# FFN gate/up stage: the second row half follows the first by seven matmuls instead of nine

## The chip, the cores and the metric

The kernel runs on one core of one Trainium2 chip. Times are device microseconds (us) of that core. A "before" and an "after" are compared only within the same rounds on the same chip, since the kernel before reads 508.7 us in one set of rounds and 509.1 us in two others.

## The reference, cut to what matters

```python
h  = x + irfft2(rfft2(layernorm(x)) * (w_r + 1j * w_i))          # opening stage, about 80 us
h2 = h + (gelu(layernorm(h) @ w_gate) * (layernorm(h) @ w_up)) @ w_down   # FFN, the rest
# x: 2048 x 576, w_gate and w_up: 576 x 4608, w_down: 4608 x 576, bf16
```

## The kernel before

The change touches only the gate/up stage of the FFN. Rows of x are taken in four blocks of 512 (`tb`), the 4608 features in 36 blocks of 128 (`f`), so there are 144 FFN blocks `m`. The contraction over 576 is cut into pieces of 64 rows. Nine pieces (5 of gate, 4 of up) run on array rows 0-63, the first half; the other nine (4 of gate, 5 of up) run on rows 64-127, the second half. Both halves of a block add into the same two PSUM banks, one for gate, one for up.

`gu(n)` emits first-half matmul `j` of block `n` and second-half matmul `j` of block `n-1` in turn: the second half runs nine matmuls behind the first. I call one such pair a step, and the nine the distance.

```python
ASEQ = [(0, i) for i in range(4)] + [(0, 8)] + [(1, 4 + i) for i in range(4)]  # (bank, weight tile), first half
BSEQ = [(0, i) for i in range(4)] + [(1, 4 + i) for i in range(4)] + [(1, 8)]  # second half
half_done = {}

def gu(n):
    for j in range(9):
        for half, m in ((0, n), (1, n - 1)):
            if not 0 <= m < 144:
                continue
            tb, f = m // 36, m % 36
            o, wt = (ASEQ, BSEQ)[half][j]
            # ... kt, HT
            h0 = 64 * half
            b = 2 * (m % 3) + o                     # six banks: three blocks are in flight
            # the second half enters a bank only after the first half's last matmul there
            aft = [half_done[m, o]] if half and (j == 0 or j == 4) else []
            op = P.op(PE, ... t.matmul(bank(b), WGU[h0:h0 + 64, wt, ...], HT[h0:h0 + 64, kt, :], ...), w=[("PS", b)], after=aft)
            if half == 0:
                half_done[m, o] = op
    m = n - 1
    if m < 0:
        st_N(NT - 1)          # last four matmuls of the opening stage; they need ScalarE's copy GS
        # ...
        return
    # ScalarE: GL = gelu(gate bank);  VectorE: AT[f] = GL * up bank

gu(0)
for tb in range(4):
    for f in range(36):
        gu(36 * tb + f + 1)
        # ... layer norm of the next 512 rows in between
    for p in range(4):
        down(tb, p)           # AT @ w_down, 72 matmuls over the full array
```

`gu(0)` has no second half, so its nine first-half matmuls run alone; nine second-half ones run alone at the end. The `after` of a second-half matmul is a wait of TensorE on itself ("self-wait"): two per block, 288 in all. It sits on the weight load that precedes the matmul.

## Time and profile before

| | before |
|---|---|
| median of 3 runs, us | 508.82 (508.56 to 509.06) |
| span of the profiled run, us | 506.9 |
| TensorE busy | 98% |
| gate/up matmuls in the chain that ended last | 56% |
| down projection in it | 28% |

The first line of the profile page, and its engine table: busy us, share of the span, instructions (PE is TensorE, PEld its weight loads). Below, the head of the chain of work that ended last, by line.

```profile
span 506.9 us, 9999 instructions
## 1 busy us (share of the span) xinstructions
PE 496.6 (98%) x4331; PEld 290.1 (57%) x4331; DVE 182.4 (36%) x376; ACT 157.6 (31%) x296; POOL 46.1 (9%) x61
...
PE PS L740 56%; PE PS L761 28%; PE PS L634 2%; PE PS L649 2%; DMA XO<-in_A_x_dram 1%; PE PS L541 1%; PE PS L579 1%; DVE T_80 L563 1%; ACT U L476 1%; DVE CUS L547 1%; PE PS L558 1%; DVE CUS L548 1%; DVE T_81 L564 1%; DVE U L474 1%; ACT JNK L411 0%
```

The same chain in order of time, its end: start, duration, what ran. L740 is gate/up, L761 down.

```profile
78.62 0.75 PE PS L634 x6
79.87 2.04 PE PS L740 x9
81.91 0.60 PE PS L649 x4
82.51 70.04 PE PS L740 x648
152.55 35.39 PE PS L761 x288
...
398.78 70.04 PE PS L740 x639
468.82 35.40 PE PS L761 x288
```

From 79.87 us to the last matmul the chain is TensorE alone. The `x9` piece is the nine lone matmuls: 2.04 us for half the work of nine steps. Each later stretch holds 648 matmuls, 324 pairs, in 70.04 us, or 216 ns a pair (the last one is 315 pairs and the nine lone second-half matmuls). A lone matmul takes the same 216 ns, so a lone matmul wastes half of its step.

The waits of the weight loads between 79 and 480 us: waiter, released by, us in total, times, longest.

```profile
PEld PS L761 <- issue: 1.7, 4, 0.4
PEld PS L740 <- issue: 1.2, 5, 0.2
PEld PS L649 <- issue: 0.4, 1, 0.4
PEld PS L740 <- ACT GL L752: 0.2, 1, 0.2
```

One weight load waited 0.2 us for ScalarE. No matmul was late for it.

### The profile page before, as it was taken

To read this page: it belongs to the slowest core of one execution; us is meant where nothing else is said; L and a number is where in the kernel's file an instruction comes from. 1 tells how busy PE (TensorE), PEld (TensorE's weight loads), DVE (VectorE), ACT (ScalarE), POOL (GpSimd) and SP (SyncE) were. 2 spreads that over 40 slices of the span, in tenths; PEclk is the share of its full clock that TensorE was granted. 3 is DMA by queue.
4 is the path that set the end of the run, shared out by engine and by line. 5 is a ranking of instruction groups with operands and counts; after the bars stand their busy time and mean duration, and the time that the engine had idled before them with its cause. 6 is when DMAs were issued, how large, how long until landed. Compare 5 with 4: busy or idle time off the path is not lost.

```text
span 506.9 us, 9999 instructions
## 1 busy us (share of the span) xinstructions
PE 496.6 (98%) x4331; PEld 290.1 (57%) x4331; DVE 182.4 (36%) x376; ACT 157.6 (31%) x296; POOL 46.1 (9%) x61
## 2 busy tenths in 40 slices
PE   6899999999999999999999999999999999999997
PEld 2578675444447774444467744444577644444776
DVE  4899673335331114443311134433211233333111
ACT  5788776663230002333310023232200132323000
POOL 3278860000000000000000000000000000000000
PEclk9899999999999999999999999999999999999999
DMA  8679798001100000100000001100000000000000
GB/s 298 151 231 321 246 334 297 1 1 23 25 9 14 17 19 14 23 19 1 1 7 17 19 12 23 25 5 1 1 19 17 13 1 1 1 1 1 13 18 19
DMA packets 25660, 28.64 MB, mean 57 GB/s; under 512 B 11408, under 2 KB 19600, under 8 KB 25488
## 3 DMA queue, kind: packets, MB, share of 16 engines
q1 hardware_dynamic: 23040, 17.39, 11.9%
q0 software_dynamic: 2576, 10.62, 6.3%
q8 instruction: 34, 0.56, 0.5%
q14 instruction: 10, 0.08, 0.1%
HBM read 23.66 MB, written 2.36 MB: 51 GB/s over the span
## 4 chain that ended last, share of the span: by engine, by line
PE 90%; DVE 4%; ACT 2%; DMA 1%; issue 1%; POOL 0%; SPq 0%; DVEq 0%; POOLq 0%
PE PS L740 56%; PE PS L761 28%; PE PS L634 2%; PE PS L649 2%; DMA XO<-in_A_x_dram 1%; PE PS L541 1%; PE PS L579 1%; DVE T_80 L563 1%; ACT U L476 1%; DVE CUS L547 1%; PE PS L558 1%; DVE CUS L548 1%; DVE T_81 L564 1%; DVE U L474 1%; ACT JNK L411 0%
## 5 line engine op out<-in xcount | busy, mean ns | idle before, releaser
L752 ACT ACTIVATE GL<-PS 128x512 bf16<-128x512 f32 x144 | 85.9, 597 | 289.9 <-PE PS L740 289.9
L753 DVE TENSOR_TENSOR AT<-GL,PS 128x512 bf16<-128x512 bf16 x144 | 98.8, 687 | 174.3 <-PE PS L740 172.6
L740 PE MATMUL PS<-HT_69,WGU 64*128 64x512 bf16 x1296 | 144.4, 376 | 0.0
L740 PE MATMUL PS<-HT_84,WGU 64*128 64x512 bf16 x1296 | 144.4, 376 | 0.0
L761 PE MATMUL PS<-WD,AT 128*128 128x288 bf16 x1152 | 141.8, 286 | 0.0
L761 PEld LDWEIGHTS PS<-WD,AT 128*128 128x128 bf16 x1152 | 112.4, 98 | 29.9 <-issue 1.7
L740 PEld LDWEIGHTS PS<-HT_84,WGU 64*128 64x128 bf16 x1296 | 64.5, 94 | 77.9 <-issue 0.5
L740 PEld LDWEIGHTS PS<-HT_69,WGU 64*128 64x128 bf16 x1296 | 64.5, 94 | 76.8 <-issue 0.7
L764 DVE TENSOR_TENSOR OS<-PS,XO 128x288 bf16<-128x288 f32 x32 | 14.6, 457 | 126.0 <-PE PS L761 126.0
L652 DVE SCALAR_TENSOR_TENSOR XO<-PS,XO 128x576 bf16<-128x576 f32 x16 | 12.1, 756 | 11.3 <-PE PS L649 11.3
L541 PE MATMUL PS<-FT,U 128*128 128x290 bf16 x96 | 14.4, 287 | 0.4 <-DVE U L474 0.4
L634 PE MATMUL PS<-DT,V 128*128 128x289 bf16 x96 | 14.5, 287 | 0.2 <-DVE V L587 0.2
L579 PE MATMUL PS<-VT,ZS 128*128 128x256 bf16 x96 | 12.9, 272 | 0.4 <-POOL ZS L568 0.2
L585 ACT ACTIVATE V<-PS 128x768 bf16<-128x768 f32 x15 | 12.0, 810 | 1.1 <-PE PS L579 0.7
L558 PE MATMUL PS<-CUS,BT 128*128 128x289 bf16 (+2 forms) x96 | 10.7, 247 | 1.4 <-DVE CUS L548 1.0
L564 DVE TENSOR_TENSOR T_81<-YS,WS 128x580 bf16<-128x580 bf16 x16 | 11.9, 746 | 0.0
L636 ACT ACTIVATE GS<-PS 128x578 bf16<-128x578 f32 x16 | 10.3, 652 | 5.0 <-PE PS L634 4.9
L561 ACT ACTIVATE YS<-PS 128x578 bf16<-128x578 f32 x16 | 10.5, 654 | 4.5 <-PE PS L558 2.8
L568 POOL TENSOR_TENSOR ZS<-T_81 128x290 bf16<-128x290 bf16 x13 | 11.6, 894 | 1.9
L452 PE MATMUL PS<-ZD 128*128 128x512 bf16 x30 | 10.4, 501 | 1.3 <-POOL ZD L369 1.3
L418 DVE BATCH_NORM_STATS2 ST_53<-XO 128x6 f32<-128x288 bf16 x24 | 9.4, 442 | 4.4 <-DMA XO<-in_A_x_dram 4.4
L541 PEld LDWEIGHTS PS<-FT,U 128*128 128x128 bf16 x96 | 9.2, 98 | 2.9 <-issue 0.8
(61 smaller groups left out, 189.8 us busy)
## 6 DMA issues: line engine op xcount, KB each, us to landing
WD<-in_B_w_down_dram POOLq DMA_DIRECT2D x9, 576.0 KB, 19.7
WGU<-in_B_w_up_dram SPq DMA_DIRECT2D x4, 1152.0 KB, 12.5
WGU<-in_B_w_gate_dram POOLq DMA_DIRECT2D x4, 1152.0 KB, 10.1
out_dram<-OS SPq DMA_DIRECT2D x32, 72.0 KB, 1.6
XO<-in_A_x_dram SPq DMA_DIRECT2D x3, 576.0 KB, 7.7
IT<-c_itab SPq DMA_DIRECT2D x1, 1024.0 KB, 6.7
HT_84<-HN SPq DMA_TRANSPOSE x40, 2.4
XO<-in_A_x_dram SPq DMA_DIRECT2D x2, 288.0 KB, 3.1
```

The costliest lines, as they stand in the source:

```text
L541: P.op(PE, lambda t, b=b, o=o, dt=dt, us=us, g=g: t.matmul(bank(b, 0, 128, 0, 2 * HK), U[:, us, g, :, :], FT[:, o, dt, :], start=(dt == 0) ...
L558: P.op(PE, lambda t, b=b, tb=tb, pl=pl, q0=q0, q1=q1, m=m, sl=sl, sp_=sp_: t.matmul(bank(b, 0, 128, q0, q1), BT[:, sp_, tb, :], CUS[:, sl, ...
L564: P.op(DVE, lambda v, g=g, sl=sl: v.tensor_tensor(T2[:, sl, :, :], YS[:, sl, :, :], WS[:, g, 1::-1, :], op=ALU.mult), r=[("Y", sl)] + wk, ...
L579: P.op(PE, lambda t, b=b, o=o, c=c, zp=zp, sl=sl, sp_=sp_: t.matmul(bank(b, 0, 128, o, o + 256), ZS[:, sl, zp, 128 * c:128 * c + 128], VT[ ...
L585: P.op(ACT, lambda a, g=g, src=src: a.activation(V[:, :, :, g, :], src, ACTF.Copy), r=rk, w=[("V", g, 0)])
L634: P.op(PE, lambda t, b=b, h=h, i=i, kt=kt, c=c: t.matmul(bank(b, 0, 128, 0, K2), V[:, kt, c, :, :], DT[:, 3 * h + i, 0:K2], start=(i == 0) ...
L652: P.op(DVE, lambda v, x2=x2, c=c, sl=sl: v.scalar_tensor_tensor(x2, banks(4 + 2 * sl, 2, 288), 1.0, x2, op0=ALU.mult, op1=ALU.add, accum_o ...
L740: op = P.op(PE, lambda t, h0=h0, kt=kt, wt=wt, f=f, b=b, HT=HT, s=(half == 0 and j in (0, 5)), e=(half == 1 and j in (3, 8)): t.matmul(ban ...
L752: P.op(ACT, lambda a, s2=s2, b0=b0: a.activation(GL[:, s2, :], bank(b0), ACTF.Gelu_apprx_tanh), r=[("PS", b0)], w=[("GL", s2)])
L753: P.op(DVE, lambda v, s2=s2, b0=b0, f=f: v.tensor_tensor(AT[:, f, :], GL[:, s2, :], bank(b0 + 1), op=ALU.mult), r=[("GL", s2), ("PS", b0 + ...
L761: P.op(PE, lambda t, b=b, h=h, f=f, p=p: t.matmul(bank(b, 0, 128, 0, 288), AT[:, f, 128 * p:128 * p + 128], WD[:, f, 288 * h:288 * h + 288 ...
L764: P.op(DVE, lambda v, b=b, h=h, p=p, c=c: v.tensor_tensor(OS[:, p % 2, 288 * h:288 * h + 288], bank(b, 0, 128, 0, 288), XO[:, c, 288 * h:2 ...
```

## The change

The intent is to shorten the start, in which the first half runs without a partner, by two steps. The sequence of steps is now numbered through, and the second half takes the step of the first half seven numbers earlier.

```diff
+    LAG = 7
     half_done = {}

     def gu(n):
-        for j in range(9):
-            for half, m in ((0, n), (1, n - 1)):
+        for s_ in range(9 * (n - 1) + LAG, 9 * n + LAG):
+            for half in range(2):
+                m, j = divmod(s_ - LAG * half, 9)
                 if not 0 <= m < 144:
                     continue
```

## The prediction

> **What bounds the kernel now.** TensorE. The engine table gives it 98% of 506.9 us, and the chain of waits is 56% gate/up matmuls of the FFN (L740) and 28% down projection (L761). In the timeline the gate/up stage runs as pairs: a matmul on rows 0-63 (first half) and one on rows 64-127 (second half) start 4 ns apart, and the next pair follows 216 ns after; 324 pairs take 70.04 us without a gap. The list of waits has one of 0.2 us for ScalarE in this stage, and it delayed only a weight load, not a matmul. The granted clock is 1.00.
>
> **What the change does.** The work is the same: 2 x 1296 gate/up matmuls, the same evictions and semaphores. Only the distance between the halves of a block shrinks from nine steps to seven, so the sequence has 144x9+7 = 1303 steps in place of 1305. The saved steps are unpaired first-half matmuls of block 0: nine stand alone now (79.80 to 81.75 us in the timeline), seven will. Nothing hides there: the four matmuls that follow need ScalarE's copy, which ends at 80.06 us, before seven are over (79.80 + 7x0.216 = 81.31). All gate/up weights have landed by then. So the gain is 2 x 216 ns = 0.43 us, all on the critical path, since TensorE waits for nothing from there to the end.
>
> **What it might add.** Before the second half may start on a bank, the first half's last matmul there must have completed, since both row tiles write that bank (the Trainium skill, TensorEngine Tiling (Array Packing), Restrictions and Gotchas: different row tiles cannot access one PSUM bank simultaneously; no run here shows it). There are 288 such self-waits. The awaited matmul is five steps ahead now and will be three. The wait sits on the weight load, which starts one step early, 2 x 216 + 6 = 438 ns after the awaited matmul started. In the trace the semaphore comes at most 395 ns after such a start, and a waiting weight load starts 43 ns after its semaphore: 438 ns. The slack of some 430 ns falls to about zero. But a late weight load is forgiven: at 113.43 us one started 111 ns behind its slot, waiting for ScalarE, and its matmul kept the 216 ns beat. So I expect no stall in the matmuls. The first half's waits for ScalarE and VectorE gain two steps of slack.
>
> **Prediction.** 508.82 - 0.43 = 508.4 us; eight times in ten between 508.0 and 508.9. Chances: faster by over 2% 0.004, within 2% 0.985, slower by over 2% 0.011.
>
> **What would show it.** Seven lone gate/up matmuls (about 1.6 us) before the last four of L649; later gate/up stretches still 70.04 us for 648 matmuls, down stretches still 35.4 us; no TensorE wait at L740 of any size in the list of waits; weight loads with the self-wait at most a few ns later than their neighbours; a span near 506.5 us.
>
> **What would make it wrong.** If a blocked wait also holds back the instructions behind it, so that the lead is not rebuilt, each self-wait could cost some 10 ns: 288 x 10 ns = 2.9 us (0.6%), and the stretches would grow from 70.04 to about 70.8 us. A stall of 36 ns per wait would be needed for 2% slower. If something other than TensorE set the pace at the start, the 0.43 us would vanish.

## The result, and the profile after

| | before | after |
|---|---|---|
| median, us (4 runs each) | 508.70 (508.56 to 509.06) | 508.25 (508.11 to 508.38) |
| ratio | | 0.9990 (95%: 0.9973 to 1.0007) |
| span of the profiled run, us | 506.9 | 506.2 |

Ratios here are the mean time of one kernel's runs over the mean of the other's runs of the same rounds, so they are not quite the ratio of the medians quoted. The verdict is "same" within 2%, and these four runs alone don't separate the two kernels: the interval takes in 1. The traces do. The head of the page after (L742 is now gate/up, L763 down):

```profile
span 506.2 us, 9998 instructions
## 1 busy us (share of the span) xinstructions
PE 495.0 (98%) x4330; PEld 289.6 (57%) x4331; DVE 182.6 (36%) x376; ACT 157.6 (31%) x296; POOL 45.9 (9%) x61
```

The end of its chain in order of time:

```profile
78.39 0.75 PE PS L634 x6
79.63 1.61 PE PS L742 x7
81.24 0.60 PE PS L649 x4
81.84 70.04 PE PS L742 x648
151.88 35.39 PE PS L763 x288
...
398.11 70.04 PE PS L742 x641
468.15 35.40 PE PS L763 x288
```

Seven lone matmuls take 1.61 us where nine took 2.04; the stretches of 70.04 and 35.39 us are unchanged. The waits of the weight loads between 79 and 480 us:

```profile
PEld PS L763 <- issue: 1.7, 4, 0.4
PEld PS L742 <- issue: 1.2, 5, 0.2
PEld PS L649 <- issue: 0.4, 1, 0.4
```

The wait for ScalarE is gone, and no self-wait has come in.

The opening stage is noise for this question: over the ten profiles the first gate/up matmul starts anywhere between 79.1 and 80.0 us where nothing before it was changed. So I also use a measure that leaves it out, worked out from the recorded starts: from the start of the last L634 matmul (shortly before this part of the program; only L649 matmuls stand between) to the start of the last matmul of all. I call it the tail interval. It is 424.830 us before and 424.398 us after: 432 ns less, which is 2 x 216 ns. A second profile of the changed kernel (below) gives 424.398 again.

### The profile page after: what moved, and what is told of

The parts are those of the page before. It is cut to its first block, busy times and chain, and to the rows that moved or that the text cites. A ratio compares the mean times of both kernels' runs of the same rounds, so it can differ in the third digit from the quotient of the medians.

```text
span 506.2 us, 9998 instructions
## 1 busy us (share of the span) xinstructions
PE 495.0 (98%) x4330; PEld 289.6 (57%) x4331; DVE 182.6 (36%) x376; ACT 157.6 (31%) x296; POOL 45.9 (9%) x61
## 4 chain that ended last, share of the span: by engine, by line
PE 88%; DVE 6%; ACT 2%; issue 1%; DMA 1%; SPq 0%; DVEq 0%
PE PS L742 56%; PE PS L763 28%; PE PS L634 2%; PE PS L649 2%; DVE T_80 L563 1%; DVE CUS L547 1%; DMA XO<-in_A_x_dram 1%; DVE T_81 L564 1%; DVE CUS L548 1%; ACT U L476 1%; DVE U L474 1%; ACT JNK L411 0%; PE PS L558 0%; ACT YS L561 0%; ACT JNK L413 0%
## 5 line engine op out<-in xcount | busy, mean ns | idle before, releaser
L742 PE MATMUL PS<-HT_69,WGU 64*128 64x512 bf16 x1296 | 143.6, 376 | 0.0
L742 PE MATMUL PS<-HT_84,WGU 64*128 64x512 bf16 x1296 | 143.6, 376 | 0.0
L763 PE MATMUL PS<-WD,AT 128*128 128x288 bf16 x1152 | 141.8, 286 | 0.0
L763 PEld LDWEIGHTS PS<-WD,AT 128*128 128x128 bf16 x1152 | 112.4, 98 | 29.9 <-issue 1.7
L742 PEld LDWEIGHTS PS<-HT_84,WGU 64*128 64x128 bf16 x1296 | 64.2, 94 | 77.6 <-issue 0.5
L742 PEld LDWEIGHTS PS<-HT_69,WGU 64*128 64x128 bf16 x1296 | 64.1, 94 | 76.8 <-issue 0.7
L634 PE MATMUL PS<-DT,V 128*128 128x289 bf16 x96 | 14.5, 287 | 0.2 <-DVE V L587 0.2
```

Source lines behind the costliest of these rows:

```text
L634: P.op(PE, lambda t, b=b, h=h, i=i, kt=kt, c=c: t.matmul(bank(b, 0, 128, 0, K2), V[:, kt, c, :, :], DT[:, 3 * h + i, 0:K2], start=(i == 0) ...
L742: op = P.op(PE, lambda t, h0=h0, kt=kt, wt=wt, f=f, b=b, HT=HT, s=(half == 0 and j in (0, 5)), e=(half == 1 and j in (3, 8)): t.matmul(ban ...
L763: P.op(PE, lambda t, b=b, h=h, f=f, p=p: t.matmul(bank(b, 0, 128, 0, 288), AT[:, f, 128 * p:128 * p + 128], WD[:, f, 288 * h:288 * h + 288 ...
```

## The experiments

Theory A: the time goes down by 216 ns for each lone step removed, and the self-waits cost nothing as long as their release comes in time. Rivals: B, the difference is chance in the opening stage; C, the nearer self-waits do cost something and hide part of a larger gain. The kernels of experiments 1, 2, 3 and 8 ran together, with nine runs of the kernel before (median 509.10 us); those of experiments 4 to 7 followed (before: 509.09 us).

### 1. The changed kernel again

No edit.

> The changed kernel itself, five rounds, for a tighter interval. Theory A (two lone pair steps of 216 ns fall away at the start, the nearer self-waits cost nothing): 0.43 us under the kernel before, so a ratio of 0.9992 and about 508.3 us. Rival B (the difference seen is chance in the opening stage, up to 80 us, whose start moved by some 0.2 us between two profiles): a mean difference nearer to 0 or to 0.2 us, with an interval that takes in 0.

Measured: 508.66 us (508.17 to 509.15), ratio 0.9990 (0.9978 to 1.0003). The run times again don't exclude 0. The tail interval does: 424.398 us against 424.830. The kernel's own runs differ by 1 us, the tail interval of two profiles by nothing at the resolution of 1 ns, so B is wrong as to the cause and right that the run times can't show it.

### 2. Distance 6

```diff
-    LAG = 7
+    LAG = 6
```

> Distance 6. The self-wait's semaphore and the weight load behind it now come 438 ns after the awaited matmul, 216 ns behind the slot of that weight load and just after its matmul was due (436 ns). Theory A1 (the two row tiles run as two streams, started in program order; a late second-half matmul shifts its own stream once by 10 to 100 ns and the first half keeps its beat): gate/up stretches stay at 70.04 us for 648 matmuls, second-half matmuls start 10 to 110 ns after their partners instead of 4, and the time is 0.1 to 0.2 us under distance 7. Theory A2 (each late weight load holds both tiles): 288 waits at 10 to 100 ns, 3 to 28 us slower, stretches of 70.8 to 77 us.

Measured: 508.36 us, ratio 0.9985 (0.9973 to 0.9998). Tail interval 424.228 us: 602 ns under before, 170 ns under distance 7. The chain:

```profile
79.76 1.40 PE PS L742 x6
81.16 0.60 PE PS L649 x4
81.76 70.05 PE PS L742 x648
```

The recorded starts of the gate/up stage show what happens at a self-wait (us; "waits" is a weight load that carries the self-wait, "signals" a matmul that increments TensorE's semaphore; the other weight loads are left out, and which half a matmul belongs to is told by the order of the program):

```
200.303  matmul       first half   (signals)
200.318  matmul       second half
200.519  matmul       first half
200.534  matmul       second half  (signals: a bank complete)
200.735  matmul       first half
200.735  weight load  second half  (waits)
200.750  matmul       second half
200.951  matmul       first half
200.966  matmul       second half
```

The load is released 432 ns after the awaited matmul, 201 ns behind its usual place, and its matmul starts 15 ns behind its partner. But the next first-half matmul still comes 216 ns after the last, and the second half simply stays 15 ns behind for the rest of the stretch (in 1254 pairs of the trace the two starts are 15 ns apart). A late second half costs its lateness once per stretch, not 288 times: 12 ns more than the usual 3, in four stretches, is about the 46 ns by which the saved step falls short of 216. That is A1, and A2 (3 to 28 us) is out.

### 3. The nearer wait without the saved steps

```diff
-    LAG = 7
+    LAG = 9
...
-                aft = [half_done[m, o]] if half and (j == 0 or j == 4) else []
+                aft = [half_done[max(k for k in half_done if k <= s_ - 3)]] if half and (j == 0 or j == 4) else []
...
-                    half_done[m, o] = op
+                    half_done[s_] = op
```

> Distance 9 as before, but each self-wait is put on the first-half matmul three steps ahead instead of five: the nearer wait alone, without the saved steps. Theory A: the same time as before to 0.1 us, nine lone matmuls at the start. If the nearer wait cost anything (rival C: it costs, and the saved steps hide that), this kernel is slower than before by 288 times that cost; 1 ns each would be 0.3 us.

Measured: 509.23 us, ratio 1.0003 (0.9990 to 1.0016); tail interval 424.830 us, to the nanosecond that of before. The nearer wait alone costs nothing, so C is out. The chain has the nine lone matmuls again:

```profile
80.03 2.04 PE PS L742 x9
82.07 0.60 PE PS L649 x4
```

### 4. Distance 5

```diff
-    LAG = 7
+    LAG = 5
```

> Distance 5. Distance 6 showed that the halves run as two streams: its second-half matmul started 447 ns after the awaited one (weight load at 432, matmul 15 later) and the first half kept its beat. At distance 5 only one first-half matmul stands in program order between the awaited one and the waiting one, so the first-half matmul after it, due at 432 ns, cannot start before about 450. Theory A1 with starts in program order: 288 waits at 15 to 20 ns, 4.3 to 5.8 us more than a kernel with the same number of steps, so about 512 to 514 us, with stretches near 71.2 us. If the first half could overtake the waiting one, no cost: about 508 us. If every late weight load held both tiles for all of its lateness, some 230 ns each: 66 us.

Measured: 515.47 us, ratio 1.0125 (1.0111 to 1.0139). Tail interval 431.368 us. That is 6.54 us over before although four steps (0.86 us) are saved, so the 288 waits cost 7.40 us, 25.7 ns each on average. The sign and the mechanism were as expected; the size was over the 15 to 20 ns. The chain in order of time, then the longest line of the waits of the weight loads between 79 and 480 us:

```profile
79.20 1.18 PE PS L742 x5
80.98 71.89 PE PS L742 x648
152.87 35.39 PE PS L763 x288
```

```profile
PEld PS L742 <- PE PS L742: 96.8, 284, 0.3
```

Two things are to be read here. The list of waits of the matmuls has no entry at all for this stage, because the matmul records, 376 ns long with modelled ends, overlap here and leave no gap; the wait shows only on the weight loads. And of the 96.8 us (0.34 us each) that they waited, only 7.4 us reached the time. The recorded starts name the terms of the 7.40 us. At one self-wait the first half starts at 202.091, 202.319, 202.547 and 202.762 us, so 228, 228 and 215 ns apart. The first 12 ns are the matmul right behind the waiting one. The second 12 (11 on average over the trace) belong to the pair after it, which also comes late; its weight loads were issued only 11 ns after the start of the delayed pair, while the usual one is 2 ns after, and the stage's first pair, started in the same way, also took 222 to 226 ns. The third term is not paid per wait: early in each stretch the second half falls back by a whole step and then starts beside the next first-half matmul, so that one first-half matmul stands alone there (81.789 us in the first stretch) and one second-half matmul at the stretch's end (152.494 us). One more step in each of four stretches is 0.86 us, which leaves 6.54 us, or 23 ns for each wait. I had left out the second and the third term.

### 5. Distance 4

```diff
-    LAG = 7
+    LAG = 4
```

> Distance 4: the waiting matmul comes directly behind the awaited one in program order. Theory A1: the next first-half matmul, due at 216 ns, starts at about 450: 288 waits at about 235 ns, 67 us more, about 575 us, with stretches near 87 us. If the first half could overtake: about 508 us.

Measured: 585.07 us, ratio 1.1490 (1.1474 to 1.1506). Tail interval 500.821 us, so with five steps saved (1.08 us) the waits cost 77.1 us, 268 ns each on average instead of the expected 235; 0.86 us of it is again one more step in each stretch. A stretch takes 89.3 us, the time between two down stretches:

```profile
171.06 35.39 PE PS L763 x288
295.71 35.39 PE PS L763 x288
```

At one of the waits, pairs start at 231.068, 231.538 and 231.764 us: 470 and 226 ns in place of 216 and 216, which is 264 ns: 254 and then 10. What made the first part larger than expected is for the most part in the semaphore: here two matmuls of one pair both signal, the two updates come 390 and 421 ns after their matmuls' starts (34 ns apart), and the waiting load needs the second.

### 6. Distance 9 with the wait of distance 5

The edit of experiment 3 with `s_ - 1` in place of `s_ - 3`.

> Distance 9 with each self-wait on the first-half matmul just one step ahead: the wait of distance 5 without its saved steps. Theory A1: the same 4.3 to 5.8 us as distance 5 above a kernel without the cost, so about 513 to 515 us, stretches near 71.2 us. If the cost at distance 5 came from something else in the order (bank pairs, evictions), this kernel stays at the time of before.

Measured: 516.30 us, ratio 1.0146 (1.0132 to 1.0159); tail interval 432.211 us, 7.38 us over before, 25.6 ns per wait on average. That is over the expected 4.3 to 5.8 us by the terms found at distance 5; the extra step in each stretch is here too. The stretches are those of distance 5:

```profile
82.43 71.89 PE PS L742 x648
154.32 35.39 PE PS L763 x288
```

So the cost at distance 5 comes from the wait alone, not from another pairing of banks or from the evictions; and the two parts add up: 432.211 - 431.368 = 0.843 us against four steps of 0.216 = 0.863.

### 7. Distance 13

```diff
-    LAG = 7
+    LAG = 13
...
-        for s_ in range(9 * (n - 1) + LAG, 9 * n + LAG):
+        for s_ in range(9 * (n - 1) + LAG if n else 0, 9 * n + LAG):
...
-            b = (6, 7, 2, 3)[2 * (p % 2) + h]
+            b = (6, 7, 4, 5)[2 * (p % 2) + h]
```

> Distance 13, away from the change's direction; the down projection uses banks 4, 5 in place of 2, 3 so that no open block is overwritten. Theory A: four lone steps more than before, 0.86 us. The same four steps are taken from the slack of the first half's waits for ScalarE and VectorE: at block 13 of the first row block, where ScalarE loads its tables twice, the weight load was already 0.1 us late at distance 9, so 0.7 to 0.9 us of TensorE waiting should appear there. Together 1.6 to 1.8 us above before, about 510.8 us. Rival: steps alone, 0.86 us; or no dependence on the number of steps, 0.

Measured: 509.99 us (509.71 to 510.87), ratio 1.0026 (1.0012 to 1.0039); the median is under the expected 510.8, the ratio is 1.3 us by the means. The tail interval, 426.444 us, is 1.61 us over before, as expected: four steps are 0.86 us, and one gap of 953 ns between pairs in place of 216 is 0.74 us. The chain shows where:

```profile
79.26 2.91 PE PS L742 x13
82.17 0.60 PE PS L649 x4
82.77 27.32 PE PS L742 x252
110.18 0.69 DVE AT L755
111.72 1.28 ACT L754
113.02 0.61 ACT GL L754
113.67 39.89 PE PS L742 x368
188.94 70.04 PE PS L742 x648
```

A larger distance leaves fewer steps between a bank's eviction and its next use. ScalarE's table loads (1.28 us each) delay one gelu, and with four steps less of slack TensorE has to wait. At distance 9 the same event only made a weight load late.

### 8. No lone steps at all

Experiments 4 to 7 together with experiments 2 and 3 say what the order has to respect: the two halves of a bank must be at least two steps apart, and up to distance 9 nothing else about the distance costs time but the lone steps (beyond it the evictions' slack does, experiment 7). So blocks can go in twos. While the first half does block 2k, the second half does block 2k+1; then they swap. Each bank's halves are five or six steps apart, and no half ever runs alone. Eight banks replace six. (The edit is shown against the changed kernel.)

```diff
-        for s_ in range(9 * (n - 1) + LAG, 9 * n + LAG):
+        for s_ in range(18):
             for half in range(2):
-                m, j = divmod(s_ - LAG * half, 9)
+                m, j = 2 * k + (s_ // 9 + half) % 2, s_ % 9
...
-                b = 2 * (m % 3) + o
-                aft = [half_done[m, o]] if half and (j == 0 or j == 4) else []
+                b = 2 * (m % 4) + o
+                lead = (m % 2 == half)
+                aft = [half_done[m, o]] if not lead and j in ((0, 5), (0, 4))[half] else []
... start and stop flags follow lead; gelu and product of both blocks after the 18 steps
-            b = (6, 7, 2, 3)[2 * (p % 2) + h]
+            b = 2 * p + h
...
-    gu(0)
+    st_N(NT - 1)
...
-            gu(36 * tb + f + 1)
+            if f % 2 == 0:
+                gu2(18 * tb + f // 2)
```

> A version without any lone step: blocks go in twos over 8 banks; while the first half does block 0, the second half does block 1, then they swap, so each bank's two halves are five or six steps apart and 1296 steps remain. Nothing is left to fill the wait for ScalarE's copy before the last four matmuls of L649, so some 0.3 us of idle TensorE comes in there. Theory A: seven steps (1.51 us) less than distance 7, less the 0.3 to 0.4 us of idle time, so about 1.1 us under distance 7 and 1.55 us under the kernel before: about 507.1 us. If steps were not the unit (B), no such gain. If the evictions, which now come in twos, free banks too late, waits of TensorE on ScalarE or VectorE appear in the gate/up lines and stretches grow beyond 70.04 us.

Measured: 507.57 us (506.94 to 508.03), ratio 0.9967 (0.9954 to 0.9981), the fastest kernel and clear of the kernel before, though far inside 2%. Tail interval 423.108 us: 1.72 us under before, 1.29 us under distance 7, where 1.55 and 1.1 were expected. The end of the chain in order of time, then the list of TensorE's waits between 76 and 480 us:

```profile
78.94 0.76 PE PS L634 x6
79.72 0.66 ACT GS L636
80.43 0.67 PE PS L649 x4
81.10 70.04 PE PS L740 x648
...
397.37 70.04 PE PS L740 x648
```

```profile
PE PS L649 <- ACT GS L636: 0.3, 1, 0.3
```

There is no piece of lone matmuls, every stretch has 648, and what is paid for it is one wait of 0.3 us for ScalarE's copy that the lone matmuls used to cover (nine steps are 1.94 us, so 0.22 us net was paid).

## Why the prediction was right

- **The gain.** Predicted 2 x 216 ns = 0.43 us, all on the critical path. The tail interval shrank by 0.432 us, the lone piece from 2.04 to 1.61 us. The medians moved by 0.45 us (508.70 to 508.25), and 508.25 lies in 508.0 to 508.9. That the medians agree so closely is in part luck, since runs of one kernel differ by 0.3 to 1.2 us; the tail interval is the evidence.
- **Nothing hid at the start.** Predicted from the copy that ends at 80.06 us. After the change the first of the four L649 matmuls still starts 308 ns after the last lone one, as before; only with no lone matmul at all (experiment 8) did the copy cost 0.3 us.
- **Self-waits with almost no slack cost nothing.** Predicted 438 ns on both sides. At distance 7 a signalling first-half matmul started at 200.156 us, its semaphore came at 200.546, and the waiting load started at 200.593, 437 ns after the matmul and 2 ns after the record before it, as its neighbours do; over the trace the self-waiting loads start 1 to 3 ns after the record before them. A blocked load started 432 ns after the awaited matmul in experiment 2, so some 5 ns of slack were left here. Experiment 3 confirms it without the saved steps.
- **A late weight load is forgiven.** Predicted from a single case of 111 ns. Experiment 2 shows it for 201 ns, with the price: 15 ns behind the partner, once per stretch. The prediction did not say that a late second half leaves the first half's beat alone; it is the reason that the cost does not recur.
- **What would have made it wrong** was named as a blocked wait that holds back the instructions behind it. That is real, but it starts two steps further down: at distance 5 it costs some 23 ns per wait and at distance 4 some 265 ns, and one step per stretch in both. The Trainium skill, TensorE: Matmul & The Clock Gate, Part 3 (The mechanism), says that matmuls start and end strictly in program order, while weight loads of another row group are pulled ahead of matmuls in flight. The starts at distances 5 and 4 agree: the first-half matmul behind a waiting second-half one started 3 or 4 ns after it (202.316 and 202.319 us at distance 5, 231.538 and 231.541 us at distance 4), never before it. But they don't show that the order of the matmuls alone did it. The first-half matmul's own weight load, usually 2 ns behind the start before it (202.091 us), was issued at 202.315 us, 3 ns behind the waiting load at 202.312; in 283 of the 285 such waits recorded at distance 5 the next load came 3 or 4 ns behind the waiting one. So a waiting weight load holds back the weight loads behind it, the other half's too, and no run here tells this from the order of the matmuls.
- **Two steps of slack for the evictions**, predicted as a by-product, were worth nothing here, since no matmul had been late. Experiment 7 shows the same slack from the other side: four steps less cost 0.74 us at the one place where ScalarE loads tables.

By distance, from the tail intervals less the steps' 216 ns each: 13: 0.74 us of waiting; 9 and 7: none; 6: under 0.05 us; 5: 7.4 us; 4: 77 us. No kernel ran at 8. Of the distances tried 6 is the best by the tail interval (the run times don't separate it from 7), and the change stopped one step short of it.

That the two halves must not write one bank at once was taken from the Trainium skill (TensorEngine Tiling (Array Packing), Restrictions and Gotchas). It was not tried here: taking the self-wait away would have been a race.

## What to carry to other kernels

Where two row tiles share a bank, count in program order how many matmuls stand between the last one that a wait needs and the one that waits. If the release (here some 435 ns after the awaited matmul starts) comes before the other tile's next matmul is due, the wait is free; one matmul fewer, and every wait held up both tiles here. A pipeline's lone start and end can also be removed altogether by letting the two halves work on two different blocks and swap, instead of one trailing the other.

## What the Trainium skill lacked or had wrong

- TensorE: Matmul & The Clock Gate, Part 2 (Back-to-back issue gap) gives about 131 ns per matmul as the sustained rate of a stream of weight loads and matmuls at N=512, and says that N/2.4 + 2.5 over-counts there. Here the nine lone 64-row matmuls at N=512, each with its own weight load, came every 216 ns (after a first gap of 226), which is what the formula gives (215.8); pairs on two row tiles also came every 216 ns, 108 per matmul.
- The same page, Part 3, gives about 4 ns between the starts of concurrent tiles; this agrees (3 to 4 ns). It doesn't say that a late tile can stay behind the other without slowing it: at distance 6 it started 15 ns behind in 1254 pairs.
- No page gives the distance in matmuls at which one matmul may wait for another on the same engine. Here the semaphore came mostly 385 to 395 ns after the start of a 64-row N=512 matmul (421 where two matmuls of a pair signalled), a blocked self-waiting weight load started 41 or 42 ns after it, and two steps of 216 ns were enough while one step cost some 23 ns per wait and one more step per stretch.
- No page says whether a weight load that waits for a semaphore holds back the other row tile's weight loads. Here it did: at distance 5 the next load came 3 or 4 ns behind the waiting one in 283 of 285 waits.
- The same page, Part 3 (The cost: per-tile semaphore tail), fits 26.3 ns per increment of concurrent tiles and 4.7 ns per tile, so 31 ns for a second tile that signals (an estimate from that fit). At distance 4 the two increments of one pair came 34 ns apart (231.458 and 231.492 us), which is near it.
